# Two more tiles of x transposed by DMA instead of by the matmul engine, with the transposes moved ahead of the plain loads

## The chip, the cores and the metric

The kernel runs on one core of one Trainium2 chip. The metric is device time in microseconds (us) of one execution; most executions of one kernel agree within about 0.3% (0.5 us of 168). The profile is one execution recorded by the hardware profiler. PE is the matmul engine (PEld its weight loads), DVE the vector engine, ACT the scalar engine, SP the engine that issues most DMAs ("SPq" is its queue).

## The reference, cut to what matters

```python
x = A_x                                        # 2048 x 512, bf16
qkv = x @ wqkv                                 # q, k, v; 32 heads of 16
phi = lambda t: where(t > 0, t + 1, exp(t)) + 1e-6
kv  = einsum("bhsd,bhse->bhde", phi(k), v);  z = phi(k).sum(over s)
a   = (phi(q) @ kv) / (phi(q) @ z) @ wo        # linear attention
h   = layernorm(x)                             # the same x (input B_x is not used)
b   = gelu(h^T @ w1 + b1) @ w2 + b2            # MLP over the tokens
out = g * a + (1 - g) * b                      # g = sigmoid(x . gate_w)
```

For the keys the kernel also needs x transposed (`xT`, features on the partitions), which is an operand of the kacc matmuls.

## The kernel before

x is cut into 16 tiles of 128 tokens. The first stage computes, tile by tile, keys (`kacc`, 4 matmuls), phi of the keys (`pk`), and accumulates `gacc` = x^T pk (4 matmuls, in four PSUM banks) and later `zacc`, the sum of pk over all tokens. The rest of the kernel (`uacc`, `qacc`, then `yps`) starts when this stage is done.

```python
    for i in range(2):                      # opening: x tiles 0-3 and wk, on two queues
        load_x(nc.sync, 2 * i, 1); load_x(nc.scalar, 2 * i + 1, 1)
    for i in range(2):
        load_wk(nc.sync, 2 * i);   load_wk(nc.scalar, 2 * i + 1)
    NPE = 6                                 # tiles 0-5 are transposed by PE
    load_x(nc.sync, 4, 2)
    for t0, n in ((NPE, 2), (8, 4), (12, 4)):
        load_xT(t0, n)                      # DMA with transpose=True, HBM -> xT
        load_x(nc.sync, t0, n)
    ...
    def transpose_tile(t, on_act):          # 4 PE transposes into PSUM, one copy to xT
        ...                                 # copy by ACT (on_act) or by DVE
    def phi(dst, acc):
        e = work.tile([P, SC], BF16, name="e", tag="e", bufs=6)
        nc.scalar.activation(out=e[:], in_=acc[:], func=ACT.Exp)
        nc.vector.tensor_scalar(...)        # min(e, 1) + 1e-6
        nc.vector.scalar_tensor_tensor(...) # max(acc, 0) + e  -> pk
    def z_tile(t):                          # 32 columns of PE; four tiles side by side
        g = t % 4
        mm(zacc[32*g : 32*g+32, :], zsel[:], pk[:, t, :], t < 4, t >= NT - 4,
           tile_position=(0, 32 * g))
    ...
    HEADS = 4
    for k in range(ND - 1):
        for t in range(HEADS): k_part(t, (k,))
    for t in range(HEADS):
        k_part(t, (ND - 1,))
        if t == 1: transpose_tile(HEADS, False)          # tile 4, copied by DVE
    for t in range(HEADS): k_phi(t)
    LAG = 4
    for t in range(HEADS, NT):
        k_part(t, range(ND))                             # kacc of tile t
        if t + 1 < NPE: transpose_tile(t + 1, True)      # tile 5, copied by ACT
        k_phi(t)
        g_tile(t - LAG)                                  # gacc of tile t - 4
        if t > LAG: ln_step(t - LN_LAG)                  # layer-norm statistics on DVE
        ...
    zacc = bank("zacc")
    for t in range(NT - LAG, NT):
        g_tile(t)
        if t == NT - 3:                                  # after gacc of tile 13
            for u in range(NT): z_tile(u)
```

The kernel divides PSUM, the memory that matmuls write to, into 8 banks of one rotating pool. Four are held by `gacc`, so four are left for `kacc`, and `kacc` of a tile can't start before the instruction that makes `pk` of four tiles earlier has read its bank.

Of the kernel before, what the change touches and what calls it, by code (L numbers as in the profile page):

```python
# [15 lines left out]
def kernel(  # L16
# [13 lines left out]
    nc = tc.nc  # L30
# [36 lines left out]
    def bank(name, dtype=FP32):  # L67
        return ps.tile([P, SC], dtype, name=name, tag="bank")
# [55 lines left out]
    def load_x(q, t0, n):  # L124
        q.dma_start(out=xs[:, t0 : t0 + n, :], in_=x_view[:, t0 : t0 + n, :])  # L125

    def load_wk(q, k):
        q.dma_start(out=wk_sb[:, k, :], in_=wqkv_view[:, k, D : 2 * D])

    def load_xT(t0, n):  # L130
        nc.sync.dma_start(
            out=xT[:, :, t0 * P : (t0 + n) * P], in_=X[t0 * P : (t0 + n) * P, :], transpose=True
        )
# [4 lines left out]
    for i in range(2):  # L138
        load_wk(nc.sync, 2 * i)
        load_wk(nc.scalar, 2 * i + 1)  # L140
    NPE = 6
    load_x(nc.sync, 4, 2)
    for t0, n in ((NPE, 2), (8, 4), (12, 4)):
        load_xT(t0, n)
        load_x(nc.sync, t0, n)
    nc.sync.dma_start(out=wq_sb[:], in_=wqkv_view[:, :, 0:D])
# [30 lines left out]
    def load_small():  # L177
        nc.gpsimd.dma_start(out=brow[0:NF, :], in_=B_b1.rearrange("(f q) -> f q", q=P))
        nc.gpsimd.dma_start(out=brow[NF : NF + NT, :], in_=B_b2.rearrange("(f q) -> f q", q=P))
        nc.gpsimd.dma_start(  # L180
            out=gw_b[:], in_=gate_w.rearrange("(o d) -> o d", o=1).to_broadcast([P, D])
        )
# [11 lines left out]
    def transpose_tile(t, on_act):  # L194
        pt = bank("pt", BF16)
        for k in range(ND):
            nc.tensor.transpose(pt[:, k * P : (k + 1) * P], xs[:, t, k * P : (k + 1) * P], ident[:])  # L197
        dst = xT[:, :, t * P : (t + 1) * P]
        src = pt[:].rearrange("p (k s) -> p k s", k=ND)
        if on_act:  # L200
            nc.scalar.activation(out=dst, in_=src, func=ACT.Copy)
        else:
            nc.vector.tensor_copy(out=dst, in_=src)  # L203
# [13 lines left out]
    def k_part(t, ks):  # L217
        if t not in kaccs:
            kaccs[t] = bank("kacc")
        for k in ks:  # L220
            mm(
                kaccs[t][:], xT[:, k, t * P : (t + 1) * P], wk_sb[:, k, :],
                k == 0, k == ND - 1,
            )

    def k_phi(t):
        phi(pk[:, t, :], kaccs.pop(t))
# [11 lines left out]
    def ln_shift(g):  # L239
        s = slice(g * TPC, (g + 1) * TPC)  # L240
        nc.vector.scalar_tensor_tensor(  # L241
            out=nmr[:, s], in0=mv[:, s, 0], scalar=-1.0, in1=rstd[:, s],
            op0=ALU.mult, op1=ALU.mult,
        )

    def ln_apply(t):
        nc.scalar.activation(  # L247
            out=hs[:, t, :], in_=xs[:, t, :], func=ACT.Identity,
            scale=rstd[:, t : t + 1], bias=nmr[:, t : t + 1],
        )  # L250
# [3 lines left out]
    def g_tile(t):  # L254
        if not gacc:
            gacc.extend(bank("gacc") for _ in range(ND))
        for k in range(ND):
            mm(gacc[k][:], xs[:, t, k * P : (k + 1) * P], pk[:, t, :], t == 0, t == NT - 1)
# [18 lines left out]
    def ln_step(u):  # L277
        ln_stats(u)
        if u % TPC == TPC - 1:
            ln_rstd(u // TPC)  # L280

    HEADS = 4
# [9 lines left out]
            k_part(t, (k,))  # L292
    for t in range(HEADS):
        k_part(t, (ND - 1,))
        if t == 1:
            transpose_tile(HEADS, False)
    for t in range(HEADS):
        k_phi(t)
    LAG = 4
# [1 line left out]
    APPLY = 9  # L301
    for t in range(HEADS, NT):
        k_part(t, range(ND))
        if t + 1 < NPE:
            transpose_tile(t + 1, True)
        k_phi(t)
        g_tile(t - LAG)
        if t > LAG:
            ln_step(t - LN_LAG)
        if t == TPC - 1 + LN_LAG:  # L310
            load_small()
        if t >= APPLY:
            ln_apply(t - APPLY)
        if t % TPC == 0 and t >= 2 * TPC:
            ln_shift(t // TPC - 2)
# [190 lines left out]
```

## Time and profile before

| | before |
|---|---|
| time | 168.21 us, median of 3 runs (167.87 to 168.40) |
| PE busy | 97% of the span |
| DVE busy | 48% of the span, but without a gap of more than 0.04 us from 9.5 to 35 us |

From the page of the kernel before (part 1: busy time; part 4: the chain of waits that ended last):

```profile
span 166.4 us, 2105 instructions
...
PE 161.7 (97%) x806; PEld 74.9 (45%) x806; DVE 80.2 (48%) x190; ACT 59.0 (35%) x91; POOL 18.2 (11%) x37
...
PE 94%; DMA 3%; DVE 1%; SPq 0%; issue 0%
```

PE carries the kernel, so a change helps only if it takes work or a wait from PE. Where PE still loses time is seen in the timeline. Columns are start, duration, engine, source line, operation, output<-inputs, count. PE, kernel before, around tiles 4 and 5:

```profile
8.62 0.60 PE L109 MATMUL kacc<-wk_sb,xT 128*128 128x512 bf16 x2
9.05 0.39 PE L197 MATMUL pt<-ident,xs 128*128 128x128 bf16 x4
9.27 1.72 PE L109 MATMUL kacc<-wk_sb,xT 128*128 128x512 bf16 x6
10.83 0.39 PE L197 MATMUL pt<-ident,xs 128*128 128x128 bf16 x4
11.05 1.23 PE L109 MATMUL gacc<-pk,xs 128*128 128x512 bf16 x4
12.12 0.38 PE L109 MATMUL kacc<-wk_sb,xT 128*128 128x512 bf16 x1
```

Matmuls are pipelined and their ends are modelled, so the distance between starts is the cost, not the duration: a matmul of 512 columns takes 0.216 us, four transposes take 0.22 us together (9.05 to 9.27). Six kacc matmuls and no wait would take 1.30 us; they take 1.56 (9.27 to 10.83), because kacc of tile 4 waits for the DVE copy. Four gacc matmuls take 1.07 us instead of 0.86 before kacc of tile 5 (12.12), which waits for ACT's copy: the trace has the wait one matmul earlier, the fourth gacc starts at 11.90, 0.05 us after the copy's end. The same stretch on DVE, kernel before:

```profile
9.47 0.42 DVE L203 COPY xT<-pt 128x512 bf16<-128x512 bf16 x1 [2.11 <-PE pt L197]
9.81 0.28 DVE L208 TENSOR_SCALAR e<-e 128x512 bf16<-128x512 bf16 x1
10.13 0.69 DVE L211 SCALAR_TENSOR_TENSOR pk<-kacc,e 128x512 bf16<-128x512 f32 x1
10.74 0.28 DVE L208 TENSOR_SCALAR e<-e 128x512 bf16<-128x512 bf16 x1
11.06 0.69 DVE L211 SCALAR_TENSOR_TENSOR pk<-kacc,e 128x512 bf16<-128x512 f32 x1
```

The bracket tells how long the engine had been idle and who ended it. After 9.47 no DVE line up to 35 us has a bracket: DVE has a backlog from here to the end of the stage. The end of the stage on PE, kernel before, all 16 zacc matmuls:

```profile
32.92 1.05 PE L109 MATMUL zacc<-pk,zsel 128*32 128x512 bf16 x16
```

The line of DVE that makes `pk` of tile 15, kernel before:

```profile
32.81 0.69 DVE L211 SCALAR_TENSOR_TENSOR pk<-kacc,e 128x512 bf16<-128x512 f32 x1
```

It ends at 33.50.

### The profile page before, as it was taken

To read this page: it belongs to the slowest core of one execution; us is meant where nothing else is said; L and a number is where in the kernel's file an instruction comes from. 1 tells how busy PE (TensorE), PEld (TensorE's weight loads), DVE (VectorE), ACT (ScalarE), POOL (GpSimd) and SP (SyncE) were. 2 spreads that over 40 slices of the span, in tenths; PEclk is the share of its full clock that TensorE was granted. 3 is DMA by queue.
4 is the path that set the end of the run, shared out by engine and by line. 5 is a ranking of instruction groups with operands and counts; after the bars stand their busy time and mean duration, and the time that the engine had idled before them with its cause. 6 is when DMAs were issued, how large, how long until landed. Compare 5 with 4: busy or idle time off the path is not lost.

```text
span 166.4 us, 2105 instructions
## 1 busy us (share of the span) xinstructions
PE 161.7 (97%) x806; PEld 74.9 (45%) x806; DVE 80.2 (48%) x190; ACT 59.0 (35%) x91; POOL 18.2 (11%) x37
## 2 busy tenths in 40 slices
PE   7999999999999999999999999999999999999992
PEld 3544444444544444444444444444444444444461
DVE  1569999986986769992301504051222121111121
ACT  3272474827658557222222111051111222111110
POOL 5000602100020000002712521000000000000000
PEclk9999999999999999999999999999999999999999
DMA  5999999999700001910597499931100000110001
GB/s 155 257 181 274 345 352 347 348 349 338 186 0 2 0 0 55 357 33 32 188 293 194 140 336 274 313 127 64 35 32 32 32 33 32 47 51 32 32 32 32
DMA packets 28953, 24.78 MB, mean 149 GB/s; under 512 B 6736, under 2 KB 28368, under 8 KB 28944
## 3 DMA queue, kind: packets, MB, share of 16 engines
q1 hardware_dynamic: 26928, 21.76, 45.0%
q0 software_dynamic: 1440, 2.38, 5.0%
q10 hardware_dynamic: 576, 0.52, 1.0%
q8 instruction: 6, 0.10, 0.3%
q14 instruction: 3, 0.02, 0.0%
HBM read 21.11 MB, written 2.23 MB: 140 GB/s over the span
## 4 chain that ended last, share of the span: by engine, by line
PE 94%; DMA 3%; DVE 1%; SPq 0%; issue 0%
PE uacc L109 29%; PE yps L109 29%; PE gacc L109 8%; PE qacc L109 8%; PE aps L109 8%; PE kacc L109 8%; DMA wk_sb<-in_A_wqkv_dram 3%; PE zacc L109 1%; PE denps L109 1%; PE kvps L109 1%; PE wps L109 1%; SPq L125 0%; DVE ot L471 0%; PE pt L197 0%; DVE xT L203 0%
## 5 line engine op out<-in xcount | busy, mean ns | idle before, releaser
L109 PE MATMUL uacc<-hs,w1c 128*128 128x512 bf16 x224 | 52.0, 379 | 0.0
L109 PE MATMUL yps<-uT,w2c 128*128 128x512 bf16 (+1 forms) x238 | 51.0, 367 | 0.0
L109 PEld LDWEIGHTS <-w2c 128*128 128x128 bf16 x238 | 23.3, 98 | 25.3
L109 PEld LDWEIGHTS <-w1c 128*128 128x128 bf16 x224 | 21.7, 98 | 26.3 <-issue 0.4
L471 DVE SCALAR_TENSOR_TENSOR ot<-yps,c,a_sc 128x512 bf16<-128x512 f32 (+1 forms) x17 | 12.1, 719 | 42.2 <-PE yps L109 41.2
L456 ACT ACTIVATE a_sc<-aps,c,gg 128x512 f32<-128x512 f32 x16 | 12.3, 777 | 46.8 <-PE aps L109 38.9
L418 DVE TENSOR_TENSOR pqT<-pqT,rex 128x512 bf16<-128x512 bf16 x16 | 6.6, 425 | 26.6 <-DMA rex<-rd_dram 26.5
L337 ACT ACTIVATE uT<-uacc,bcol 128x512 bf16<-128x512 f32 x14 | 9.3, 687 | 27.5 <-PE uacc L109 27.5
L109 PE MATMUL kacc<-wk_sb,xT 128*128 128x512 bf16 x64 | 16.1, 379 | 0.5 <-DMA wk_sb<-in_A_wqkv_dram 0.4
L109 PE MATMUL aps<-W2sb,pqT 128*128 128x512 bf16 x64 | 16.4, 379 | 0.0
L109 PE MATMUL qacc<-xT,wq_sb 128*128 128x512 bf16 x64 | 16.4, 379 | 0.0
L109 PE MATMUL gacc<-pk,xs 128*128 128x512 bf16 x64 | 16.1, 380 | 0.0
L247 ACT ACTIVATE hs<-xs,nmr,rstd 128x512 bf16<-128x512 bf16 x16 | 12.8, 804 | 2.5 <-DVE nmr L241 2.5
L207 ACT ACTIVATE e<-qacc 128x512 bf16<-128x512 f32 x16 | 9.6, 597 | 10.2 <-PE qacc L109 10.2
L207 ACT ACTIVATE e<-kacc 128x512 bf16<-128x512 f32 x16 | 9.1, 593 | 8.9 <-PE kacc L109 8.9
L208 DVE TENSOR_SCALAR e<-e 128x512 bf16<-128x512 bf16 x32 | 9.1, 284 | 6.3 <-ACT e L207 6.3
L211 DVE SCALAR_TENSOR_TENSOR pk<-kacc,e 128x512 bf16<-128x512 f32 x16 | 11.1, 692 | 0.6
L211 DVE SCALAR_TENSOR_TENSOR pqT<-qacc,e 128x512 bf16<-128x512 f32 x16 | 11.1, 692 | 0.5
L416 POOL DMA_DIRECT2D rex<-rd_dram x16 | 9.4, 597 | 16.6 <-DVE pqT L418 14.9
L231 DVE BATCH_NORM_STATS2 stats<-xs 128x6 f32<-128x512 bf16 x16 | 10.9, 682 | 0.0
L404 DVE CUSTOM_DVE_ANT_0 junk<-xs,gw_b 128x512 bf16<-128x512 bf16 x16 | 9.9, 688 | 0.0
L109 PEld LDWEIGHTS <-xT 128*128 128x128 bf16 x64 | 6.1, 98 | 8.2 <-issue 0.9
(66 smaller groups left out, 67.6 us busy)
## 6 DMA issues: line engine op xcount, KB each, us to landing
w2c<-in_B_w_dram SPq DMA_DIRECT2D x4, 1792.0 KB, 9.8
w1c<-in_B_w_dram SPq DMA_DIRECT2D x2, 2048.0 KB, 16.1
w1c<-in_B_w_dram SPq DMA_DIRECT2D x3, 1024.0 KB, 11.3
rex<-rd_dram POOLq DMA_DIRECT2D x16, 128.0 KB, 6.6
out_dram<-ot SPq DMA_DIRECT2D x15, 128.0 KB, 1.7
xs<-in_A_x_dram SPq DMA_DIRECT2D x2, 512.0 KB, 4.0
xs<-in_A_x_dram SPq DMA_DIRECT2D x2, 256.0 KB, 4.4
wq_sb<-in_A_wqkv_dram SPq DMA_DIRECT2D x1, 512.0 KB, 6.0
```

The lines of the kernel that those rows point to most:

```text
L109: nc.tensor.matmul(o, lhsT=lhsT, rhs=rhs, start=start, stop=stop, **kw)
L207: nc.scalar.activation(out=e[:], in_=acc[:], func=ACT.Exp)
L208: nc.vector.tensor_scalar(out=e[:], in0=e[:], scalar1=1.0, scalar2=PHI_EPS, op0=ALU.min, op1=ALU.add)
L211: nc.vector.scalar_tensor_tensor(out=dst, in0=acc[:], scalar=0.0, in1=e[:], op0=ALU.max, op1=ALU.add)
L231: nc.vector.bn_stats(out=stats[:], in_=xs[:, t, :])
L247: nc.scalar.activation(out=hs[:, t, :], in_=xs[:, t, :], func=ACT.Identity, scale=rstd[:, t : t + 1], bias=nmr[:, t : t + 1],)
L337: nc.scalar.activation(out=uT[:, j, :], in_=acc[:], func=ACT.Gelu_apprx_tanh, bias=bcol[:, j : j + 1])
L404: nc.vector.tensor_tensor_reduce(out=junk[:], in0=xs[:, t, :], in1=gw_b[:], scale=1.0, scalar=0.0, op0=ALU.mult, op1=ALU.add, accum_out=gp ...
L416: nc.gpsimd.dma_start(out=rex[:], in_=src.unsqueeze(1).to_broadcast([8, HEAD, SC]))
L418: nc.vector.tensor_tensor(out=seg, in0=seg, in1=rex[:], op=ALU.mult)
L456: nc.scalar.activation(out=a_sc[:], in_=aps[:], func=ACT.Identity, scale=gg[:, t : t + 1], bias=c2[:, t : t + 1],)
L471: nc.vector.scalar_tensor_tensor(out=ot[:, :W], in0=yps[:, :W], scalar=c1[:, t : t + 1], in1=a_sc[:, cs], op0=ALU.mult, op1=ALU.add,)
```

## The change

Its evident intent is to take the last two PE transposes with a copy behind them out of PE's way in the middle of the stage, and to start the transposing DMAs earlier so that they land in time.

```diff
-    NPE = 6
-    load_x(nc.sync, 4, 2)
-    for t0, n in ((NPE, 2), (8, 4), (12, 4)):
+    load_xT(4, 2)
+    load_xT(6, 2)
+    load_x(nc.sync, 4, 4)
+    for t0, n in ((8, 4), (12, 4)):
         load_xT(t0, n)
         load_x(nc.sync, t0, n)
@@
         k_part(t, (ND - 1,))
-        if t == 1:
-            transpose_tile(HEADS, False)
@@
         k_part(t, range(ND))
-        if t + 1 < NPE:
-            transpose_tile(t + 1, True)
         k_phi(t)
```

## The prediction

> **What bounds the kernel.** The page gives PE 97% of the span and the chain of waits is 94% PE; DMA is 3%, all of it the opening load of wk. The change acts only in the first 35 us. There the timeline shows PE starting the kacc matmuls at 6.03 us (0.4 us wait for wk) and losing time around tiles 4 and 5: four transposes start at 9.05 and the next matmul at 9.27 (0.22 us); kacc of tile 4 starts at 9.95, although two matmuls (0.216 us each) would have let it start near 9.70 (0.25 us, waiting for the 0.42 us DVE copy); four more transposes cost 0.22 us; kacc of tile 5 starts at 12.12 instead of 11.91 (0.21 us, ACT's 0.60 us copy). From there PE hardly stops. DVE runs without a gap from 9.47 to 35.0 us: the second limit.
>
> **Removed:** 8 PE transposes, one DVE copy, one ACT copy, and their waits: 0.90 us of PE's line at most.
>
> **What takes half of it back.** gacc of tile 0 needs pk of tile 0, the end of a chain whose start does not move: kacc 0, exp at 9.03 (0.59), DVE min/add, DVE max/add. Without the DVE copy in its way DVE's part moves only from 9.81 to about 9.67, so pk 0 ends near 10.68 (was 10.82) and pk 1 near 11.61. PE would reach gacc 0 at about 10.35 and wait until 10.72; kacc 5, which by the built order waits on DVE (I read it as pk 1 releasing a PSUM bank), starts about 11.66 instead of 12.12. Net gain: 0.45 us. DVE's saturated chain is earlier by only 0.14 us: pk 15 ends at about 33.36 (was 33.50), and the last zacc matmul, now at 33.85, would want it at 33.4. That just fits; perhaps 0.05 us is lost. I expect 0.4 us to survive to the end.
>
> **DMA side.** The two-tile transpose of before is issued at 4.22, holds the issuing queue 1.48 us and lands 4.3 us after issue, at 8.5. The new first one takes the slot of the plain load at 3.79: landing about 8.0, needed about 9.45. The second is issued about 5.3, lands about 9.5 to 10.5, needed about 13.4. The first four-tile transpose lands near 14 (needed 16.8). Plain tiles 4 to 7 land near 11.5, needed near 17.5. Weights come about 1 us later; w1c is needed at 35 and lands near 27. So no landing should end a wait. The Trainium skill, "VectorE: DVE Perf Modes", section on the three transpose paths, gives 390 ns for a 128x128 transpose on TensorE and 1309 ns by DMA; pipelined in this trace TensorE's costs only 55 ns, so little TensorE time is to be won.
>
> **Predicted:** 167.8 us against 168.21; range 167.2 to 168.6. Faster by over 2%: 0.01; within 2%: 0.97; slower by over 2%: 0.02.
>
> **What would show it.** Timeline: kacc 4 at about 9.5, no wait for a transpose; gacc 0 waiting on DVE until about 10.7; kacc 5 near 11.65; first uacc near 35.2 (was 35.64). Issues: first transpose landing by 9 us. Wrong if a kacc wait for a DMA transpose appears in the waits view, or wk lands later than 6.0.
>
> **What would make it wrong.** The present first four-tile transpose stalls about 1 us in mid-transfer (DMA traffic near zero from 9.5 to 10.3 us); such a stall in the new first transpose would hold kacc 4 and cost up to 1 us. Run-to-run scatter (0.5 us) is as large as the gain.

## More of the kernel before

```profile
33.59 0.39 PE L109 MATMUL zacc<-pk,zsel 128*32 128x512 bf16 x4
33.91 0.39 PE L109 MATMUL gacc<-pk,xs 128*128 128x512 bf16 x1
```

The x4 line is the last group of four of the 16 zacc matmuls, with one of them reading `pk` of tile 15.

## The result, and the profile after

| | before | changed |
|---|---|---|
| median of all runs | 168.43 us (6 runs, 167.87 to 170.44) | 168.25 us (6 runs, 167.84 to 168.52) |
| ratio of fast runs | | 0.9994, 95% interval 0.9974 to 1.0014 |

The ratio is the mean time of one kernel's fast runs over that of the other's of the same rounds, so it is not quite the ratio of the medians; the run of 170.44 us, over 1.5% above the fastest, counts as slow and is left out of it. The measured time lies in the predicted range, but so does that of the kernel before (168.43), and of the predicted gain of 0.4 us little is to be seen. From the page of the changed kernel:

```profile
span 166.4 us, 2087 instructions
...
PE 161.0 (97%) x798; PEld 74.3 (45%) x798; DVE 79.8 (48%) x189; ACT 58.3 (35%) x90; POOL 18.2 (11%) x37
...
PE 93%; DMA 3%; DVE 1%; SPq 1%; ACT 0%; issue 0%
```

PE has 0.7 us less work, and the span is the same. Timeline of PE, changed kernel, at tiles 4 and 5:

```profile
8.62 2.11 PE L109 MATMUL kacc<-wk_sb,xT 128*128 128x512 bf16 x9
10.95 1.02 PE L109 MATMUL gacc<-pk,xs 128*128 128x512 bf16 x4 [0.23 <-DVE pk L212]
11.88 0.59 PE L109 MATMUL kacc<-wk_sb,xT 128*128 128x512 bf16 x2
```

The transposes and the waits for copies are gone, kacc 4 runs straight behind the head tiles, and no wait for a transposing DMA appears. A new wait stands before gacc of tile 0, for its pk. On DVE, changed kernel:

```profile
9.88 0.29 DVE L209 TENSOR_SCALAR e<-e 128x512 bf16<-128x512 bf16 x1 [2.83 <-ACT e L208]
10.20 0.69 DVE L212 SCALAR_TENSOR_TENSOR pk<-kacc,e 128x512 bf16<-128x512 f32 x1
```

The start of both profiles differs by chance: in this profile the wk weights landed later (first kacc matmul at 6.25 us, 6.03 before), and everything behind is shifted with it. To compare, count from the first exp of a kacc on ACT, which ends that scatter: it starts at 9.03 in the profile of before and at 9.25 in the changed one. So counted, pk of tile 0 ends at 1.79 before and 1.64 after, gacc 0 starts at 2.02 and 1.70, kacc 5 starts at 3.09 and 2.63. PE is 0.45 us ahead, DVE's chain 0.15 us (starts are read to 0.01 us, so differences can be off by as much). This lead of PE reaches the end of the stage: zacc starts at 23.89 before and 23.44 after. And there most of it is lost. End of the stage on PE, changed kernel, to be set against the lines of before: all 16 zacc matmuls, the last group, and the last member of the group with what follows it:

```profile
32.69 1.31 PE L109 MATMUL zacc<-pk,zsel 128*32 128x512 bf16 x16
```

```profile
33.34 0.65 PE L109 MATMUL zacc<-pk,zsel 128*32 128x512 bf16 x4
```

```profile
33.62 0.38 PE L109 MATMUL zacc<-pk,zsel 128*32 128x512 bf16 x1
33.93 0.39 PE L109 MATMUL gacc<-pk,xs 128*128 128x512 bf16 x1
```

and the operand that this single zacc matmul needs, on DVE:

```profile
32.88 0.69 DVE L212 SCALAR_TENSOR_TENSOR pk<-kacc,e 128x512 bf16<-128x512 f32 x1
```

The other three matmuls of the last group started at 33.34 to 33.35 (24.1 from the first exp). The fourth reads pk of tile 15, which ends at 33.57, and it starts alone at 33.62, 0.27 us late. The next matmul starts 0.31 us after it, just as it starts 0.31 to 0.32 us after the members of a full group in the profile of before. So being late by 0.27 us cost 0.27 us in full: of the lead of 0.45 us about 0.19 is left for the stage after it (first uacc 26.42 us after the first exp, 26.61 before). From the first uacc to the end of the span all 14 profiles of this document take 130.75 to 130.77 us, so whatever is won or lost before the first uacc arrives at the end unchanged. The Trainium skill says in "TensorEngine Tiling (Array Packing)", Key Properties, that different tiles of the array can execute matmuls in parallel; the trace agrees, with four starting within 0.01 us, and adds that the delay of one late member is passed on in full (also 0.13 us in plain_first and 0.18 us in pe_back, each time with the next matmul 0.31 us behind the late one).

The waits view of the changed kernel does not show this wait, because the modelled ends of the earlier matmuls (0.38 us each) reach over it. Only the start times show it.

The DMA side did what was foreseen. From the view of tile xT, issue to landing of the transposing DMAs, first the kernel before (three of them, one of two tiles), then the changed one (four, two of them of two tiles):

```profile
DMA to landing us min/median/max: 4.3/5.3/6.3
```

```profile
DMA to landing us min/median/max: 3.9/4.8/5.5
```

The first new transpose was issued at 3.41 us and landed 4.4 us later, at 7.8; it is first needed at 9.7.

### The profile page after: what moved, and what is told of

Same layout as the page of the kernel before. It is cut to its first block, busy times and chain, and to the rows that moved or that the text cites. A ratio compares the mean times of both kernels' runs of the same rounds, so it can differ in the third digit from the quotient of the medians.

```text
span 166.4 us, 2087 instructions
## 1 busy us (share of the span) xinstructions
PE 161.0 (97%) x798; PEld 74.3 (45%) x798; DVE 79.8 (48%) x189; ACT 58.3 (35%) x90; POOL 18.2 (11%) x37
## 4 chain that ended last, share of the span: by engine, by line
PE 93%; DMA 3%; DVE 1%; SPq 1%; ACT 0%; issue 0%
PE uacc L109 29%; PE yps L109 29%; PE gacc L109 8%; PE qacc L109 8%; PE aps L109 8%; PE kacc L109 8%; DMA wk_sb<-in_A_wqkv_dram 3%; PE zacc L109 1%; PE denps L109 1%; PE kvps L109 1%; PE wps L109 1%; SPq L125 1%; DVE pk L212 0%; ACT e L208 0%; DVE ot L468 0%
## 5 line engine op out<-in xcount | busy, mean ns | idle before, releaser
L109 PEld LDWEIGHTS <-xs 128*128 128x128 bf16 x64 | 6.2, 98 | 8.4 <-issue 1.2
```

What stands on the lines that cost most here:

```text
L109: nc.tensor.matmul(o, lhsT=lhsT, rhs=rhs, start=start, stop=stop, **kw)
```

## The experiments

The edits are to the changed kernel unless said otherwise; the declaration of a spare tile is left out. All 12 runs gave correct results. In the expectations, theory A is that the zacc group waits for pk 15, the end of DVE's backlog. Theory B is that the gain is lost in the opening because the early transposes delay wk. Theory D is that PE is the limit of the stage. The expectations of the first eight runs count the stage from the first kacc matmul; those of the last four, and the results here, count from the first exp, because kacc turned out to wait for later wk blocks too in some profiles (3.00 or 3.01 us from first kacc to first exp in most, 3.20 in before_late_z, 3.31 in dve_back, 4.09 in early_wk).

| profile | first exp at | pk 15 ends, from first exp | first uacc, from first exp |
|---|---|---|---|
| before / again | 9.03 / 9.16 | 24.47 / 24.45 | 26.61 / 26.61 |
| changed / again / third | 9.25 / 9.15 / 9.22 | 24.32 / 24.32 / 24.32 | 26.42 / 26.42 / 26.42 |
| late_z / again | 8.88 / 8.96 | 24.32 / 24.31 | 26.15 / 26.15 |
| before_late_z | 9.01 | 24.46 | 26.61 |
| pe_back | 9.07 | 24.46 | 26.56 |
| late_z_pe_back | 9.12 | 24.46 | 26.39 |
| dve_back | 9.12 | 25.48 | 27.58 |
| dve_clean | 9.19 | 24.64 | 26.74 |
| plain_first | 8.83 | 24.30 | 26.40 |
| early_wk | 10.86 | 24.30 | 26.15 |

Repeated profiles of one kernel agree within 0.02 us in the last two columns, while the first column scatters by 0.4 us. That is why the profile can tell apart what the run times can't.

### late_z: give zacc more time, in the changed kernel

```diff
-    for t in range(NT - LAG, NT):
-        g_tile(t)
-        if t == NT - 3:
-            for u in range(NT):
-                z_tile(u)
+    for t in range(NT - LAG, NT - 1):
+        g_tile(t)
+    for u in range(NT):
+        z_tile(u)
+    g_tile(NT - 1)
```

> The changed kernel, with only the order of the last PE work of the first stage changed: gacc of tile 14 goes before the zacc matmuls, gacc of tile 15 after them. Stage length here is the time from the first kacc to the first uacc matmul: 29.61 us in the profile of before, 29.42 in that of the changed kernel. Theory A (the gain of PE is thrown away at zacc, which waits for pk of tile 15, the end of DVE's saturated chain): the 16 zacc matmuls take 1.0 us again instead of 1.31, the stage is 29.1 to 29.2 us, and the time is 0.2 to 0.3 us below the changed kernel's (about 0.998 of before). Rival B (the gain is lost in the opening, because wk lands later, and the zacc stretch is noise of one profile): the stage stays 29.4, the time that of the changed kernel.

Measured: 167.84 us median, ratio to before 0.996 (0.9946 to 0.9973). Timeline of PE at the end of the stage:

```profile
33.18 1.05 PE L109 MATMUL zacc<-pk,zsel 128*32 128x512 bf16 x16
34.16 1.04 PE L109 MATMUL gacc<-pk,xs 128*128 128x512 bf16 x4
35.03 0.81 PE L109 MATMUL uacc<-hs,w1c 128*128 128x512 bf16 x3
```

All 16 zacc matmuls run in 1.05 us again, and the stage is 26.15 us, 0.27 below the changed kernel and 0.45 below the kernel before. The whole of PE's lead comes through. This is what theory A expects and theory B excludes.

### before_late_z: the same reordering in the kernel before

> The kernel before with the same reordering of gacc 14 and zacc. Theory A: no wait stood before zacc there (its 16 matmuls took 1.05 us), so the stage stays 29.6 us and the time is that of before within 0.1%. If the reordering itself saves time (a theory C), the stage is shorter by about 0.2 us here too.

Measured: 168.49 us, ratio 1.0002 (0.999 to 1.0015), stage 26.61 as before. The reordering is worth nothing by itself; it only lets pass what the change had gained. (Counted from the first kacc it reads 29.81, because in this profile a later wk block was waited for. This made me count from the first exp.)

### pe_back: PE's work put back, without the copies

```diff
     for t in range(HEADS, NT):
+        if t < 6:
+            kaccs[t] = bank("kacc")
+            for _ in range(4):
+                mm(kaccs[t][:, :P], warm[:, 0:P], warm[:, :P], True, True)
         k_part(t, range(ND))
```

> The changed kernel with PE's removed work put back alone: four matmuls of 128 columns on constants before kacc of tile 4 and of tile 5 each (about 0.22 us each four), written to the bank that kacc then overwrites; no copy on DVE or ACT. Theory A: PE's 0.44 us fall into its waits for pk 0, pk 1 and pk 15, and the stage stays 29.4 us (within 0.07). If PE were the limit of the stage (theory D), it is 29.8 us.

Measured: 168.37 us, ratio 1.0 (0.9986 to 1.0013); stage 26.56, neither 26.42 nor the 26.86 of theory D. The 0.14 us that I had not expected came by way of DVE. In this trace pk 4 and pk 5 wait for PE's semaphore as well as for DVE's own, which they don't in the changed kernel; presumably because PE now writes their banks twice. In the profile the distance from the min/add to the max/add on DVE for these two tiles is 0.40 and 0.39 us instead of 0.32 and 0.31. That makes pk 15 later by 0.14 us, and the stage by the same 0.14. Of PE's own 0.44 us nothing shows: first uacc follows pk 15 at the distance of 2.10 us in both kernels. So this run speaks for theory A, with a side effect of the edit in it.

### late_z_pe_back: the same work where zacc does not wait

> The reordered version with the eight small PE matmuls put back. With zacc no longer waiting for pk 15, theory A says that PE is the limit of the stage from tile 5 on, so what was hidden in the changed kernel now shows: kacc 5 is later by 0.22 us and so is the first uacc, 26.37 us from the first exp instead of 26.15. If DVE still limits somewhere, it is nearer 26.15.

kacc 5 starts 0.23 us later (2.86 us from the first exp, 2.63 without the extra matmuls), and the stage grows by 0.24, to 26.39, as expected. pk 15 is as late as in pe_back, but zacc does not feel it here. The same eight PE operations take nothing from the stage by their own time while DVE is the limit, and cost 0.24 us once it is not. The other four of them hide in the wait for pk 0.

### dve_back: DVE's copy put back, without the PE transposes

```diff
     for t in range(HEADS):
+        if t == 2:
+            nc.vector.tensor_copy(out=spare[:], in_=kaccs[t][:, :320])
         k_phi(t)
```

> The changed kernel with a useless DVE copy of 128x320 from PSUM, about 0.4 us (of the removed DVE copy's 0.42), put in DVE's stream ahead of phi of tile 2, nothing on PE or ACT. Theory A: pk 15 and the stage end come later by about the copy's length, stage 29.8 us. Theory D (PE limits): the stage stays near 29.4 or grows by under 0.1.

Measured: 169.41 us, ratio 1.0051 (1.0029 to 1.0073). The stage grew by 1.16 us, not by 0.4. The timeline of ACT in this run shows why:

```profile
12.13 2.06 ACT L208 ACTIVATE e<-kacc 128x512 bf16<-128x512 f32 x4 [1.92 <-DVE spare L299]
```

The copy read the bank of kacc 2, and ACT's exp of that bank was held until the copy was done. DVE then idled 0.66 us for the exp. The edit did more than I meant. Still, pk 15 came later by 1.16 us and the first uacc by 1.16 us: what delays DVE's chain delays the stage one for one.

### dve_clean: a DVE copy that holds up nothing else

```diff
+        if t == 2:
+            nc.vector.tensor_copy(out=spare[:], in_=xs[:, 3, :])
         k_phi(t)
```

> The changed kernel with a useless DVE copy of 128x512 from SBUF ahead of phi of tile 2. The earlier run of this kind read kacc of tile 2, and ACT's exp of the same bank then waited for the copy, so the chain lost 1.15 us instead of 0.48. This copy reads x, so nothing but DVE is held up. Theory A: pk 15 and first uacc are later by just the copy's length (0.3 to 0.6 us, to be read from the profile), counted from the first exp. Theory D (PE limits): no change.

The copy takes 0.42 us by its record and 0.33 us of DVE's line (11.68 to the next start at 12.01). pk 15 is later by 0.32 us, the first uacc by 0.32. PE at the end of the stage, dve_clean:

```profile
32.62 1.04 PE L109 MATMUL zacc<-pk,zsel 128*32 128x512 bf16 x15
33.88 0.38 PE L109 MATMUL zacc<-pk,zsel 128*32 128x512 bf16 x1 [0.22 <-DVE pk L212]
34.19 1.90 PE L109 MATMUL gacc<-pk,xs 128*128 128x512 bf16 x8
```

Here the wait is long enough to come out from under the modelled ends, and the profile names it: the sixteenth zacc matmul waits for pk on DVE. The distance from the end of pk 15 to the start of this matmul is 0.05 us, as in the changed kernel.

### before_again and after_again: is the later wk landing real?

> The kernel before unchanged, for a second profile. If the wk wait is set by the order of the loads (theory B), the first kacc starts again near 6.03 us; if it scatters from profile to profile by 0.2 us, the difference of 0.22 us in the first kacc between the first two profiles says nothing about the change. Stage length 29.6 either way.

> The changed kernel unchanged, for a second profile. Theory B: first kacc near 6.25 again. Scatter: anywhere from 5.9 to 6.3. Stage 29.4, zacc stretch about 1.3 us (theory A).

The first kacc started at 6.16 in the kernel before (6.03 in its first profile) and at 6.15 in the changed one (6.25). Taking the first exp over all profiles with an unchanged opening, the three with the old order of loads have 9.01 to 9.16 (mean 9.07), the nine with the new one 8.88 to 9.25 (mean 9.11). The difference of 0.04 us is a tenth of the scatter; with three profiles against nine a shift of 0.1 us either way is not excluded. But the loss in question lies behind the first exp (26.42 against late_z's 26.15), where a late wk can't have made it. Theory B falls.

### plain_first: transposing DMAs behind the plain load

```diff
+    load_x(nc.sync, 4, 4)
     load_xT(4, 2)
     load_xT(6, 2)
-    load_x(nc.sync, 4, 4)
```

> The changed kernel with the plain load of tiles 4 to 7 issued before the two two-tile transposes, so only the order of that part is undone. The first transpose is issued about 0.6 us later and queues behind 512 KB, which I estimate at 1.7 us at the 300 GB/s of the opening: it should land about 9.5 to 10.5 us. If the order matters (the change's intent), kacc of tile 4, wanted near 9.7, waits for it and the stage grows by up to 0.5 us; as DVE still has a backlog of pk 0 to 3 then, theory A says that the stage loses less than kacc 4 waits. If the landing stays before 9.7, nothing changes.

Measured: 168.07 us, ratio 0.9967 (0.9924 to 1.0009, an interval too wide to claim anything from). PE, plain_first:

```profile
9.84 1.04 PE L109 MATMUL kacc<-wk_sb,xT 128*128 128x512 bf16 x4 [0.41 <-DMA xT<-in_A_x_dram]
10.72 1.03 PE L109 MATMUL gacc<-pk,xs 128*128 128x512 bf16 x4
```

The first transpose landed at 9.8 (4.13 plus 5.7), and kacc 4 waited 0.41 us for it. But the stage is 26.40 us, that of the changed kernel: the wait took the place of the later waits, that for pk 0 and half of that for pk 15 (the last zacc starts 0.13 us late instead of 0.27). So the reordering of the loads does remove a wait for DMA, and while DVE limits the stage this is worth nothing that these runs can show.

### early_wk: can the start be moved?

```diff
+    load_x(nc.sync, 0, 1); load_x(nc.scalar, 1, 1)
+    load_wk(nc.sync, 0)                   # wk block 0 before x tile 2
+    load_x(nc.scalar, 3, 1)
+    load_x(nc.sync, 2, 1)
+    load_wk(nc.scalar, 1); load_wk(nc.sync, 2); load_wk(nc.scalar, 3)
```

(on top of late_z, in place of the two opening loops)

> The reordered version late_z with the opening loads reordered too: wk block 0 goes before x tile 2 on SP's queue, x tile 3 stays second on ACT's. Theory A: the whole stage hangs on the first kacc, so if wk block 0 lands earlier by about 0.4 us (128 KB less ahead of it, an estimate at the opening's 300 GB/s), first uacc and the end come earlier by as much, stage length unchanged near 29.2. If x tile 2 then becomes the wait, or a later wk block, the gain is smaller and the stage longer.

Measured: 169.61 us, ratio 1.0037 (0.9982 to 1.0091): whether it is slower at all the times don't decide. The profile is clear: wk block 0 landed 2.9 us after its issue, at 4.1, but x tile 2 landed at 5.9, and PE takes tiles 2 and 3 in this order. PE, early_wk:

```profile
5.95 1.03 PE L200 MATMUL pt<-ident,xs 128*128 128x128 bf16 x8 [1.06 <-DMA xs<-in_A_x_dram]
6.77 0.63 PE L109 MATMUL kacc<-wk_sb,xT 128*128 128x512 bf16 x1
```

The first exp came at 10.86, about 1.8 us later, and the stage behind it was 26.15 us, exactly late_z's. My estimate of 0.4 us for a swapped place was wrong: what is third on its queue lands near 6 us in these profiles, x tile 2 here (5.9) as wk block 0 in the profile of before (6.0). The span of this profile is 167.8 us, against 165.8 and 165.9 of late_z, so in it the delay reached the end. The six timed runs scatter from 168.02 to 170.37 us; whether x lands that late in each of them was not looked at.

### after_timed and late_z_again: side by side on one chip

> The changed kernel unchanged, timed on the same chip as the next. Theory A: within 0.2% of before (0.998 to 1.0), stage (now counted from the first exp of kacc to the first uacc matmul, which takes the scatter of the wk landing out) 26.42 us against 26.61 of before.

> The reordered version again, beside it. Theory A: stage from first exp to first uacc 26.15 us again, 0.27 below the changed kernel's, so 0.15% to 0.2% faster than it; ratio to before 0.996 to 0.998. If the first timing (0.996) was partly chance, the ratio is nearer 0.998.

Measured: the changed kernel 168.27 us, ratio 0.9988 (0.9966 to 1.001); late_z 167.87 us, ratio 0.9972 (0.9953 to 0.9991); before 168.53 us. The stages are 26.42 and 26.15 as before. late_z beats the kernel before in both timings, with an interval below 1 each time. Against the changed kernel the time alone doesn't decide (the two intervals overlap); the two profiles of late_z and the three of the changed kernel do, with 0.27 us.

## Why the prediction was right or wrong

The range and the verdict were right: 168.25 us, within 2%. That says little for the reasoning: the range of 1.4 us also holds the time of the kernel before, so a change worth nothing would have met it. The mechanism was right in kind: PE loses 0.9 us of work and waits, DVE's chain gives half of that back at once. The size was not: 0.4 us were to survive, and the profiles show 0.19.

- **Gain at tiles 4 and 5, 0.45 us.** Right. Counted from the first exp, gacc 0 was predicted at 1.69 and starts at 1.70; kacc 5 was predicted at 2.63 and starts at 2.63. That pk 1 frees kacc 5's bank was an inference from the built order; the time of kacc 5 agrees with it (pk 1 ends at 11.82 in the changed kernel, kacc 5 starts at 11.88).
- **DVE's chain earlier by 0.14 us.** Right: 0.15.
- **"That just fits; perhaps 0.05 us is lost."** This step failed. I had spread the 16 zacc matmuls evenly up to the next matmul at 33.91 and so put the need for pk 15 at 33.85 in the profile of before. They run in groups of four that start together, and the last group starts at 33.59. With PE earlier by 0.45 us the need falls to 24.1 us after the first exp, while pk 15 is ready at 24.32 and used 0.05 us later. The term for this wait was put at 0.05 us and measures 0.27 (26.42 against 26.15 in late_z). What survives is the slack of 0.04 us that PE had here before and the 0.15 us by which DVE's chain is earlier: together the 0.19 us measured.
- **No landing ends a wait; first transpose lands about 8.0.** Right: 7.8, and no wait for it. The later transposes landed sooner than predicted (the second at 8.7 instead of 9.5 to 10.5, the first of four tiles at 12.6 instead of 14). The Trainium skill's "VectorE: DVE Perf Modes" (the three transpose paths) gives 390 ns for a 128x128 transpose on TensorE; the prediction used the trace's 55 ns for a pipelined one, from four that take 0.22 us together (9.05 to 9.27). The four stand-ins of the same 128 columns before kacc 4 in late_z_pe_back, which are no transposes, take 0.23 us.
- **First kacc unmoved.** Right on average; in the first profile of the changed kernel it was 0.22 us later by chance, which hid the small gain in that profile's span altogether. By the letter of the prediction's own test ("wk lands later than 6.0") it would have been wrong, but the kernel before fails that test too (first kacc at 6.03 and 6.16): the test was finer than the scatter.
- **Scatter as large as the gain.** Right: both ratios of the changed kernel (0.9994 and 0.9988) have intervals that contain 1.

## What to carry to other kernels

Where two engines reach a meeting point nearly together (here pk 15 was ready 0.09 us before it was used), taking work from one of them gains only as much as the other one gives, so look for the next meeting point on the way to the end and compare both arrival times there. When it turns out to be the limit, first try to move the consumer back in program order: putting four independent matmuls ahead of zacc turned 0.19 us into 0.45 us at no cost that the runs show. And count small effects inside the profile from a point behind the noisy loads, where repeats agree to 0.02 us, rather than from the run times.

## What the Trainium skill lacked or had wrong

- "TensorEngine Tiling (Array Packing)", Key Properties, says that tiles execute in parallel, but not what a late one costs: a single zacc matmul of 32 columns that missed its group of four by 0.27 us held up everything behind it by 0.27 us. The same list says that a change of tiling mode drains the TensorE, without a figure. In these runs the first matmul after such a change follows 0.31 us after the last one before it, in both directions (gacc to zacc, 32.62 to 32.92, and zacc to gacc, 33.59 to 33.91, in the profile of before), where groups of zacc follow each other at 0.22 us; no run here shows that the drain is the reason.
- "VectorE: DVE Perf Modes", the three transpose paths, gives one figure for each path (390 ns on TensorE, 1309 ns by DMA for 128x128). In these runs four TensorE transposes in a row took 0.22 us, and a DMA transpose of eight such blocks landed 3.9 to 4.4 us after its issue in the changed kernel. The table doesn't say whether its figures are latencies or rates; other pages have rates for both paths, and it doesn't point to them.
- "DMA: Bandwidth & Descriptors", Issuing engines are not separate DMA queues, calls the issue time of a DMA "usually small relative to the DMA itself". For the transposing DMAs of the kernel before it was 1.48 us of 4.3 us to landing for two tiles, and 3.25 us of 5.3 for the last four-tile one.
- "Perfetto Trace Analysis", Tensor Engine Instruction (MATMUL, LD_WEIGHTS), says that the end time of a matmul is estimated, but no page that I read says that such an end can hide a short wait: the 0.27 us before the last zacc matmul is in no wait of the changed kernel's profile.
